# A gated convolution-and-MLP kernel: an early first sine, its constants in five tasks, the gate as columns of the array, the last matrix by transfer, and four outputs finished from PSUM

## The chip, the cores and the metric

The kernel runs on one core of one Trainium2 chip. The core has TensorE (PE; its weight loads are shown apart as PEld), VectorE (DVE), ScalarE (ACT), GpSimd (POOL) and SyncE (SP), which here issues all the transfers. SBUF is the working memory of 128 partitions, PSUM the memory that PE writes to, here eight banks of 512 fp32 columns. The metric is the device time of one execution in microseconds (us), and the median of the runs counts.

## The reference

Everything works on x = A_q, 2048 tokens of 640 columns in bf16. Two branches, A and B, are mixed by a gate per token:

```python
g = sigmoid((x * gate_w).sum(-1, keepdims=True))
out = g * A(x, k, v, ...) + (1 - g) * B(x, w1, w2, w3, w4)
```

Branch A: k is shifted by 0 to 3 tokens with four weights per column and summed, multiplied by v (this is kv), and convolved along the tokens with a filter of 2048 taps per column, ssm_k, by FFTs of length 4096; kv * ssm_D is added, and the sum is multiplied by x. Branch B: layernorm, w1 (640 to 640), gelu; the four quarters of the result are shifted by 1, -1, 2 and -2 tokens; w2; the residual is added (x1). Then layernorm, w3 (640 to 1536), gelu, w4 (1536 to 640), and x1 is added.

## The kernel before

**Tasks and their order.** `build` makes 769 tasks. Each has a name, an engine or a choice of two, a function that issues its instructions, the tasks it depends on, and the buffers it takes and gives back (banks of PSUM, the pools "xn", "FS", "FX", "GX", "Q", "O", "V" and others). The text ORDER lists the tasks by number; a letter behind a number names the engine (a for ACT, v for DVE, p for POOL). The tasks are issued in that order, so it fixes the order on each engine and in SP's queue of transfers. `place` goes through the list once with the durations written at the tasks, and decides which buffer a task gets and how many filler matmuls (L256, on zeros, their result is not used) stand ahead of a PE task. The hardware waits for what a task needs, not for the planned times.

**Layout.** A token is 32 n + 16 g + s: s counts 16 blocks of 128 tokens. x lies in SBUF as 16 such blocks and is overwritten by x1 and at last by branch B's result.

**Start.** POOL writes integer ramps (task `iota`, L392), then ones, a constant and the identity matrix, and zeroes one row of K (task `ident`, L403). DVE works out the phases of all cosines and sines as integers (`phsmall`, `phase0`, `phase1`, `phand`, L417 to L456), and one ACT instruction makes TRIG from them (`sin`, L458). SP loads x, the filter (SK) and weights. For each block of x the statistics are made on DVE or ACT (`st1`), finished on POOL (`rs1`, L530), the block is normalised (`nm1`) and transposed on PE in pairs of blocks (`tr1`, L548) into xnT. PE also transposes the filter in five blocks of 32 (`trh`, L762, evicted by `evt`), and broadcasts the four shift weights over the partitions (`cjb`, L473).

**Branch B.** W1 (`w1`, L623 and L627), gelu (`g1`, L640), W2 (`w2`, L649), the residual on DVE (`x1`, L656) with its sums on ACT (`sq`), the second layernorm (`ve2` on DVE, `st2` on POOL, `nm2`), a transposing transfer per block (`dt2`, L724), W3 in four groups of four blocks (`w3`, L732, 12 pieces each), gelu (`g2`, L739), W4 (`w4`, L746: 24 matmuls per block into two banks) and the sum into x on DVE (`t2`, L752). The later parts of groups 1 to 3 serve PE as work between the steps of branch A.

**Gate.** `gate` (L666) runs 80 matmuls of one column, five per block of tokens, and five for the sum of gate_w. `gz` (L677) undoes the layernorm for the product on DVE, a tanh and `gg` turn it into the two factors GG and OG per token.

**Branch A.** `kv` (L779 to L790): 8 DVE operations on 2560 columns for each of four groups of blocks, after which group K holds the product. The FFT is written as matmuls with TRIG. Step 1 (`s1h` for the filter, `s1x` for kv, L817 and L830) goes to the buffer FS (ACT or DVE, L387 and L389) and to DRAM (FH, FXD); kv group 0 is the last to be done, its step 1 has four blocks and a rest (`s1x.0` to `s1x.3`, `s1xr.0`). Then, ten times: load FX, step 2 for both (`s2`, L864), evict, products on DVE (L879), step 3 (`s3`, L892), evict to GS, store to GD. The last step (`s4`, L936) loads GX and needs the matrix BT: TRIG's rows are reordered into BP (part of the buffer XB) by DVE (`bperm`, L910), transposed by 16 matmuls (`trb`, L917) and copied back from PSUM by DVE (`evb`).

**Output.** For a block: `yq` (L942) takes step 4 from PSUM, multiplies by GG and by x as loaded anew (QO), into a piece of W4's buffer; `ad` (L948) adds x (by then branch B's result) times OG; two blocks are stored together in two halves of 64 partitions (`st`, L382).

Of the kernel before, what the change touches and what calls it, by code (L numbers as in the profile page):

```python
# [36 lines left out]
0 60v 22 73a 1 74 7 2 21 20 23 71v 3 8 4 9 16 72 63a 5 64 61a 53v 70p 14 51v 62 12 54 79v 13a 75v 31 36 52 18 38  # L37
391 81v 6 66v 56v 24 17a 392v 32 82 89v 25 65a 15a 395 80 67 76v 30 34 90 396a 69v 387 388v 55v 77 37 83v 68a
393 47 35 57 78a 87a 84v 88 28 26 394v 389 97v 33 85 59a 86v 390v 92v 119 42 10 397 121 58a 98 27 95v 100v 113v
19 450 41 91a 93 94v 96 40 11a 99v 111v 39 400 120 451a 123 122 438 124 105v 439a 29 444 43 127 452 401 402 445a  # L40
440 441a 141 101 145 125 112 115v 398 128 102a 453a 142 146 44 149 150 442 446 106 126 443a 147 148 403 404 129
130 447a 454 405 143 114 138 139 455a 132 133 45 144 406 103a 154 155 456 458 399 157 116a 131 407 50 457a 104
107v 158 448 160 161 459a 411 449 108a 134 135 109 136 117 140 151 152 110a 118a 211 137 410 412 163 212 164 462
464 460 468 465a 463a 165 217 167 185 213v 469a 186 169 408 413 470 218 46 466 215v 409 168 221v 414 166 415 416
417 171 467a 471a 461 193 49 474 170 214 473 172 478 187 191 479a 176 177 421 472 194 475a 173 216 192 219a 480
174 220 188 420 482 189 481a 190 179 222 180 476 483a 477a 485 156 204 422 486 494 205 423 201 202 484 207 495a
490 492 424 48 208 487a 418 162 153 419 425 491a 488 489a 493a 223 496 198 224 498 199 497 500 501a 231 239 426
502 504 499a 506 232 243 503a 233 240 225 431 507a 182 427 430 432 505a 433 226 244 510 234 514 428 515a 509 183
241 434 435 436 227 511a 242 228 429 512 516 513a 518 517a 519a 508 437 237 245 238 246 255 256 209 229 195 522
524 230 235 520 196 523v 525a 236 528 529a 530 526 249 521 253 257v 531a 527v 694v 210 251 247 159 206 258 178  # L50
533 261 250 532 184 203 259v 262 260 175 265v 263v 266 264 267 197 299 252 300 181 305 306 539 540 534 254 349
200 542 343 301a 309v 248 273 555 550 307v 541v 302 571 535 268 543a 537 274 538a 287 288 556 557a 536v 279 280
582 558 544 545 551 553 559a 552v 554a 310 289 290 281 308 572 566 303v 304 344 546 573a 547a 275 583 350 351v
574 276 560 548v 347v 575a 695 561 271 598 567 584a 696v 569 353v 585 282 603 283 570v 568a 586a 311 277 604 284
606 272 576 577 599 312 607v 315 605a 587 588 278 600v 590 589a 323 578 316 549 619 591v 324 580a 601 319 614
329 602a 320 635 630 592 562 593 269 579v 330 620 564v 563a 270 678 581 345v 608 609 615 622 621a 616v 325 623a
285 326 662 286 594 596a 565 331 631 595v 617 618v 327 636 637v 632a 633 332 624 634a 625 638 346 725 321 610
640 639a 667 641 612a 328 651 291 348 663 611a 322 664a 292 626 646 628a 665 313 627v 668 669v 666a 647 314 670
648v 671a 333 652 334 597 653v 654 655a 317 318 649 650a 642 644a 672 673 656 683 339 684 657 354 643a 613 340
674 679 676v 685a 681 352 645 675a 682v 658 680a 688 686 687a 660a 337 629 689 690 659a 335 661 677 338 692v 336  # L60
691a 693 297 707 724 341 342 298 295 706 355 356 726 708 296 727 709 729 365 730 369 742 728 366 697 370 361 733
# [293 lines left out]
def build(env, nc, io):  # L355
# [36 lines left out]
    def c_iota(t):  # L392
        T = env.early("TT", [P, 16, 2], I32)
        for h in range(2):
            nc.gpsimd.iota(T[64 * h:64 * h + 64], pattern=[[1, 16], [-6144, 2]], base=6144 + 16 * h, channel_multiplier=32)
        nc.gpsimd.iota(env.early("KC", [P, 64], I32)[:], pattern=[[4, 64]], base=1, channel_multiplier=0)
        nc.gpsimd.iota(env.early("PI", [P, 1], I32)[:], pattern=[[0, 1]], base=0, channel_multiplier=1)
        nc.gpsimd.iota(env.early("K2", [P, 2, 32], I32)[:], pattern=[[0, 2], [1, 32]], base=0, channel_multiplier=0)
        nc.gpsimd.iota(env.early("N2", [P, 5, 16, 2], I32)[:], pattern=[[0, 5], [1, 16], [16, 2]], base=0, channel_multiplier=0)
        nc.gpsimd.iota(env.early("OF", [P, 5, 32], I32)[:], pattern=[[-2048, 5], [0, 32]], base=6144, channel_multiplier=0)  # L400
    add("iota", "POOL", 2.2, c_iota, w=["iota"], roles=("C0",))

    def c_id(t):  # L403
        I = env["ID"]
        nc.gpsimd.memset(env["ONE"][:], 1.0)
        nc.gpsimd.memset(env.early("NPI", [P, 1], F32)[:], float(-np.pi * (1 - 2.0 ** -20)))
        nc.gpsimd.memset(I[:], 0.0)
        nc.gpsimd.affine_select(out=I[:], in_=I[:], compare_op=ALU.not_equal, fill=1.0, base=0, pattern=[[-1, P]],
                                channel_multiplier=1)
        nc.gpsimd.memset(env.sm("MH", [P, 2])[:], -0.5)  # L410
        nc.gpsimd.memset(env["K"][0:1, 0:3, :], 0.0)
    add("ident", "POOL", 2.9, c_id, w=["ID", "c0", ("K", "z")], roles=("C0", "K"))
# [27 lines left out]
    add("phsmall", "DVE", 2.6, c_small, r=["iota"], w=["ph0"], roles=("PRE", "C0"))  # L440
# [10 lines left out]
    for ri in range(2):  # L451
        add(f"phase{ri}", "DVE", 1.25, c_ph(ri), r=["iota"], w=[("ph", ri)], roles=("PRE", "C0"))
# [8 lines left out]
    add("sin", "ACT", 3.5, c_sin, r=["pha", "c0"], w=["TRIG"], roles=("PRE", "C0"))  # L461
# [203 lines left out]

    def gate(t):  # L666
        m = env.PS[:, t.buf["U"][0], :]
        gw = env.sm("GW", [P, 5], BF16)
        for s in range(16):
            for kb in range(5):  # L670
                nc.tensor.matmul(m[:, s:s + 1], lhsT=env["xnT"][:, s + 2, kb, :], rhs=gw[:, kb:kb + 1], start=(kb == 0),
                                 stop=(kb == 4))
        for kb in range(5):
            nc.tensor.matmul(m[:, 16:17], lhsT=env["ONE"][:], rhs=gw[:, kb:kb + 1], start=(kb == 0), stop=(kb == 4))
    tg = add("gate", "PE", 2.3, gate, r=["GW", "c0"] + [("xnT", s) for s in range(16)], acq=[ONE], mode="f", roles=("xnT",))

    def gz(t):  # L677
        m = env.PS[:, tg.buf["U"][0], :]
        z, sd = SS("Z"), SS("SD")
        sg = env.sm("SG", [P, 1])  # L680
        nc.vector.tensor_tensor(out=sd[:], in0=SS("VE")[:], in1=SS("RS")[:], op=ALU.mult)
        nc.vector.tensor_scalar(out=sg[:], in0=m[:, 16:17], scalar1=-1.0, scalar2=None, op0=ALU.mult)
        nc.vector.scalar_tensor_tensor(out=z[:], in0=SS("NB")[:], scalar=sg[:, 0:1], in1=m[:, 0:16], op0=ALU.mult, op1=ALU.add)
        nc.vector.tensor_tensor(out=z[:], in0=z[:], in1=sd[:], op=ALU.mult)
    add("gz", "DVE", 0.8, gz, use=[tg], rel=[(tg, "U")], r=[("RS", s) for s in range(16)], w=["Z"])
# [7 lines left out]
    add("gg", "DVE", 0.35, gg, r=["Z"], w=["GG"])  # L693
# [9 lines left out]
    def f_st2(t, s0):  # L703
        c = slice(s0, s0 + 2)
        r, nb = SS("r2")[:, c], SS("nb2")[:, c]
# [3 lines left out]

    for c in range(4):  # L710
        nT, nP = None, f"x1nT{c % 2}"
        for s0 in (4 * c, 4 * c + 2):
# [5 lines left out]
            for s in ss:  # L718
                def f_nm2(t, s=s):
                    k = slice(s, s + 1)  # L720
                    norm(t, env["xn"][:, t.buf["xn"][0], :], env["x"][:, s, :], SS("r2")[:, k], SS("nb2")[:, k])
# [19 lines left out]
        for s in range(4 * c, 4 * c + 4):  # L741
# [6 lines left out]
            t = add(f"w4.{s}", "PE", 3.28, w4, r=["W4"] + [("h2", c, fb) for fb in range(12)], rel=[(h2, "h2")], acq=("U",), mode="f")  # L748
# [165 lines left out]
    def trb(t):  # L914
        o = env.Ub(t.buf["U"][0])
        for s in range(16):
            nc.tensor.transpose(o[:, 128 * s:128 * s + 128], env.BP[:, s, :], env["ID"][:])  # L917
    tb = add("trb", "PE", 1.65, trb, r=["BP", "ID"], acq=("U",), mode="f")
    add("evb", {"ACT": 1.87, "DVE": 1.25}, 0, lambda t: copy(t, env["BT"].rearrange("p s t -> p (s t)"), env.Ub(tb.buf["U"][0])), use=[tb],
        rel=[(tb, "U")], w=["BT"])  # L920
    for s0 in range(0, 16, 2):
# [7 lines left out]
        for i in range(2):  # L929
# [16 lines left out]

            def ad(t_, s=s, i=i, y=y, o=oown):
# [5 lines left out]
            oown = oown or o  # L953
        halves(f"st.{s0}", P * 2 * D * BF * 1.3, lambda t, g, s0=s0: ov[g, :, s0:s0 + 2, :],
# [34 lines left out]
```

## Time and profile before

| | |
|---|---|
| median of 3 runs | 234.26 us (232.64 to 235.73) |
| the profiled execution | 233.85 us |
| its span in the profile | 232.1 us |
| mean granted TensorE clock | 0.988 |
| PE, DVE, ACT, POOL busy | 220.8, 186.9, 155.1, 40.5 us |
| moved by transfers | 56.23 MB, mean 242 GB/s |

A row of groups reads: line, engine, operation, output<-input by the program's names, shape, count, then busy time and mean ns of one, then the idle time of the engine just before such an instruction and what ended it. PE's matmuls overlap, so their mean is longer than the distance from one to the next; for PE the chain of waits is the better measure: it gives for each piece of work its start and the time until the next. "PE PS L746 x24" there means 24 matmuls of line 746 writing to PSUM. A row of waits tells who waited for whom, the total, how often, and the longest. In SP's rows "SPq" is the issue of a transfer, not the transfer.

### The profile page before, as it was taken

The page shows a single profiled execution, that of the slowest core. Times are in us where ns is not written, and L with a number is a line of the kernel's source. Part 1 is how long each engine was busy: PE and PEld are TensorE (multiplying, and loading weights), DVE is VectorE, ACT ScalarE, POOL GpSimd, SP SyncE. Part 2 cuts the span into 40 slices and gives each one's busy share as a digit, 9 for nine tenths or more (in the row PEclk, how much of TensorE's full clock was granted, in tenths as well). Part 3 has the DMA queues.
Part 4 walks back from the last instruction along what each step waited for, and adds up shares of the span by engine and source line. Part 5 has one row for each costly group of instructions (what it writes and reads, how often), then busy time and mean ns, then how long its engine had stood idle before and what let it go on. Part 6 is the DMA issues. An engine that isn't in the chain of part 4 may idle for free.

```text
span 232.1 us, 5340 instructions
## 1 busy us (share of the span) xinstructions
PE 220.8 (95%) x2143; PEld 108.6 (47%) x2163; DVE 186.9 (81%) x264; ACT 155.1 (67%) x221; POOL 40.5 (17%) x90
## 2 busy tenths in 40 slices
PE   7799999999999999999999999999999999999990
PEld 3158834456345744445543433344345554444550
DVE  5974699989999989997378998897986128887972
ACT  2996989988897998979669988888956004142000
POOL 7585317810700000011340000000000000000000
PEclk9979999999999999999999999999999999999998
DMA  5899889976999696867899995899843894968742
GB/s 149 280 277 303 198 237 272 330 270 206 289 294 283 196 266 224 270 224 250 191 315 300 327 349 177 255 228 310 204 172 135 242 406 147 282 187 248 233 109 57
DMA packets 39051, 56.23 MB, mean 242 GB/s; under 512 B 13809, under 2 KB 28914, under 8 KB 39026
## 3 DMA queue, kind: packets, MB, share of 16 engines
q1 hardware_dynamic: 39026, 55.88, 81.8%
q8 instruction: 17, 0.28, 0.5%
q14 instruction: 8, 0.07, 0.1%
HBM read 34.90 MB, written 18.35 MB: 229 GB/s over the span
## 4 chain that ended last, share of the span: by engine, by line
PE 80%; DVE 7%; DMA 4%; issue 2%; SPq 2%; ACT 2%; DVEq 0%; ACTq 0%
PE PS L746 21%; PE PS L732 18%; PE PS L649 8%; PE PS L623 7%; PE PS L864 4%; PE PS L892 4%; PE PS L762 3%; DMA FX<-FH 3%; PE PS L817 3%; DVE VC L786 3%; PE PS L256 2%; PE PS L936 2%; SPq L382 2%; PE PS L627 2%; DVE VC L782 2%
## 5 line engine op out<-in xcount | busy, mean ns | idle before, releaser
L746 PE MATMUL PS<-W,h2T 128*128 128x128 bf16 (+1 forms) x374 | 53.2, 297 | 0.5
L739 ACT ACTIVATE h2T<-PS 128x512 bf16<-128x512 f32 x48 | 28.1, 609 | 30.8 <-PE PS L732 30.0
L746 PEld LDWEIGHTS <-h2T 128*128 128x128 bf16 x384 | 29.6, 98 | 25.3 <-issue 2.5
L387 ACT CAST FS<-PS 128x1024 bf16<-128x1024 f32 x38 | 37.1, 1022 | 4.5 <-PE PS L817 2.6
L732 PEld LDWEIGHTS <-W 128*128 128x128 bf16 x240 | 21.2, 98 | 30.0 <-issue 8.5
L387 ACT CAST XH<-PS 128x1024 bf16<-128x1024 f32 x26 | 25.8, 1014 | 6.5 <-PE PS L864 6.4
L732 PE MATMUL PS<-x1nT,W 128*128 128x512 bf16 x120 | 28.8, 380 | 0.0
L732 PE MATMUL PS<-XB,W 128*128 128x512 bf16 x120 | 28.6, 380 | 0.0
L752 DVE TENSOR_TENSOR x<-PS,x 128x640 bf16<-128x640 f32 x16 | 13.1, 822 | 15.8 <-PE PS L746 15.8
L879 DVE TENSOR_TENSOR PP<-XH 128x2048 bf16<-128x2048 bf16 x20 | 23.6, 1219 | 0.9 <-PE PS L892 0.4
L782 DVE TENSOR_TENSOR VC<-K,VC 128x2560 bf16<-128x2560 bf16 x16 | 23.8, 1485 | 0.2
L649 PE MATMUL PS<-W,hsT 128*128 128x128 bf16 (+1 forms) x152 | 23.1, 295 | 0.4
L623 PE MATMUL PS<-xnT,W 128*128 128x512 bf16 x80 | 19.1, 380 | 0.5 <-ACT hsT L640 0.5
L389 DVE CAST XH<-PS 128x1024 bf16<-128x1024 f32 x14 | 16.7, 1219 | 2.8 <-PE PS L864 2.7
L649 PEld LDWEIGHTS <-hsT 128*128 128x128 bf16 x160 | 12.9, 98 | 11.5 <-issue 0.2
L786 DVE TENSOR_TENSOR VC<-VC 128x2560 bf16<-128x2560 bf16 x12 | 17.9, 1489 | 0.2
L942 DVE SCALAR_TENSOR_TENSOR W<-PS,GG,QO 128x640 bf16<-128x640 f32 x16 | 13.6, 879 | 4.4 <-PE PS L936 3.9
L706 POOL TENSOR_TENSOR r<-v,MH 128x2 f32<-128x2 f32 x8 | 6.9, 856 | 55.6 <-DVE v L701 55.5
L387 ACT CAST GS<-PS 128x1024 bf16<-128x1024 f32 x13 | 13.0, 1018 | 3.1 <-PE PS L892 3.1
L656 DVE SCALAR_TENSOR_TENSOR x<-PS,x 128x640 bf16<-128x640 f32 x16 | 13.1, 820 | 2.3 <-PE PS L649 2.0
L948 DVE SCALAR_TENSOR_TENSOR QO<-x,OG,W 128x640 bf16<-128x640 bf16 x16 | 13.6, 879 | 0.1
L864 PE MATMUL PS<-FX,TRIG 64*32 64x512 bf16 x320 | 12.9, 382 | 0.1
(106 smaller groups left out, 272.4 us busy)
## 6 DMA issues: line engine op xcount, KB each, us to landing
FH<-FS SPq DMA_DIRECT2D x8, 640.0 KB, 5.4
FXD<-FS SPq DMA_DIRECT2D x8, 640.0 KB, 4.6
FX<-FXD SPq DMA_DIRECT2D x10, 512.0 KB, 5.5
FX<-FH SPq DMA_DIRECT2D x10, 512.0 KB, 5.2
GX<-GD SPq DMA_DIRECT2D x8, 640.0 KB, 5.2
W<-in_B_w_dram SPq DMA_DIRECT2D x2, 1920.0 KB, 10.5
GD<-GS SPq DMA_DIRECT2D x8, 480.0 KB, 3.8
x<-in_A_q_dram SPq DMA_DIRECT2D x16, 160.0 KB, 4.9
```

Of the source, the lines that this page charges most:

```text
L387: nc.scalar.copy(out=out, in_=in_)
L389: (nc.vector if t.on == "DVE" else nc.gpsimd).tensor_copy(out=out, in_=in_)
L623: nc.tensor.matmul(m[:, b, :], lhsT=W[:, 0, kb, 160 * fb:160 * fb + 128], rhs=rhs(kb, shifts[fb]), start=(kb == 0), stop=(kb == 4))
L649: nc.tensor.matmul(m[:, c0:c1], lhsT=env["hsT"][:, o.buf["hs"][0], fb, 128 * (s % 4):128 * (s % 4) + 128], rhs=env["W12"][:, 1, fb, c0:c1] ...
L732: nc.tensor.matmul(env.PS[:, t.buf["U"][0], :], lhsT=env["W3"][:, kb, 128 * fb:128 * fb + 128], rhs=env.nT(int(nP[-1]))[:, :, kb, :], star ...
L739: nc.scalar.activation(out=env["h2T"][:, o.buf["h2"][0], fb, :], in_=env.PS[:, t.buf["U"][0], :], func=ACT.Gelu_apprx_tanh)
L746: nc.tensor.matmul(m[:, c0:c1], lhsT=env["h2T"][:, o.buf["h2"][0], fb, 128 * (s % 4):128 * (s % 4) + 128], rhs=env["W4"][:, fb, c0:c1], st ...
L782: nc.vector.tensor_tensor(out=VC[:, o], in0=env["K"][:, a + 3 - j:a + 7 - j, :], in1=w, op=ALU.mult)
L786: nc.vector.tensor_tensor(out=VC[:, 1], in0=VC[:, 1], in1=VC[:, 2], op=ALU.add)
L864: nc.tensor.matmul(env.U(t.buf["U"][0])[32 * j:32 * j + 32, gp, :], lhsT=CRI()[64 * gp:64 * gp + 64, 32 * pc:32 * pc + 32], rhs=X[64 * gp: ...
L879: nc.vector.tensor_tensor(out=env["PP"][:, o.buf["PP"][0], a, :].rearrange("p (b c) -> p b c", b=2), in0=X.unsqueeze(1).broadcast_to([P, 2 ...
L942: nc.vector.scalar_tensor_tensor(out=u, in0=env.Uf(t.buf["U"][0])[:, 0:D], scalar=SS("GG")[:, s:s + 1], in1=env["QO"][:, 2 * q.buf["Q"][0] ...
```

## The change

- **Sine.** DVE zeroes two elements (`warm0`) and ACT takes the sine of one of them (`warm`) as the first instruction of the kernel on ACT; `sin` comes after it.
- **Constants in five tasks.** `iota` keeps the ramps that `phase0` and `phase1` read; `iotb` holds the four others, which `phsmall` reads; `ident`, `ones` and `kz` hold the identity, the ones and constants, and the zero row of K.
- **Gate as array columns.** Five matmuls with one column each become one matmul of 5 columns for the sum of gate_w (`sgm`), reduced on DVE, which also copies gate_w over 32 columns (`sg`, GB). `gate` multiplies GB with xnT: 20 matmuls of 512 columns, four of them side by side in 32 output partitions each. `gz` gets the tokens back onto the partitions with two 32x32 block transposes on DVE out of PSUM.
- **Last matrix by transfer.** `bperm` may also run on POOL, and does in the new order; `trb` and `evb` are replaced by one transposing transfer of 16 blocks (`dbt`).
- **Last four outputs from PSUM.** For blocks 12 to 15, W4 is two tasks, 512 and 128 columns, one bank each. x1 times OG is added to the piece from `yq` first (`ax`), and then one DVE step for each half takes W4's result from PSUM, times OG, plus that piece, into the output (`fo`); `t2` and `ad` are not run for these blocks. Each of the four is stored by itself.
- **Order.** ORDER has 785 tasks and is another list throughout. Some tasks stand elsewhere: the shift weights are now the first transfer, the gate weights come behind two blocks of the filter, W3 is loaded ahead of W4, W4 behind the first stores to FXD, the gate runs among W1's second half. Ahead of the first transpose of the filter PE has 15 fillers.

```diff
-    add("iota", "POOL", 2.2, c_iota, w=["iota"], roles=("C0",))
+    add("iota", "POOL", 0.65, c_iota, w=["iota"], roles=("C0",))
...
+    def c_warm(t):
+
+        nc.vector.memset(env.sm("Z", [P, 16])[:, 0:2], 0.0)
+    add("warm0", "DVE", 0.08, c_warm, w=["WA"])
+    add("warm", "ACT", 1.5, lambda t: nc.scalar.activation(out=env.sm("Z", [P, 16])[:, 1:2], in_=env.sm("Z", [P, 16])[:, 0:1], func=ACT.Sin),
+        r=["WA"], w=["WB"])
...
-        for s in range(16):
-            for kb in range(5):
-                nc.tensor.matmul(m[:, s:s + 1], lhsT=env["xnT"][:, s + 2, kb, :], rhs=gw[:, kb:kb + 1], start=(kb == 0),
-                                 stop=(kb == 4))
+        gb = env.sm("GB", [P, 5, 32], BF16)
         for kb in range(5):
-            nc.tensor.matmul(m[:, 16:17], lhsT=env["ONE"][:], rhs=gw[:, kb:kb + 1], start=(kb == 0), stop=(kb == 4))
+            for k in range(4):
+                nc.tensor.matmul(m[32 * k:32 * k + 32, :], lhsT=gb[:, kb, :], rhs=env["xnT"][:, 2:18, kb, 32 * k:32 * k + 32],
+                                 start=(kb == 0), stop=(kb == 4))
...
+        for h in range(2):
+            nc.vector.transpose(out=T, in_=env.PS[:, tg.buf["U"][0], 256 * h:256 * h + 256])
+            c = slice(8 * h, 8 * h + 8)
+            nc.vector.tensor_tensor(out=z[:, c], in0=T.rearrange("p (s j) -> p s j", j=32)[:, :, 0], in1=z[:, c], op=ALU.subtract)
...
-    add("bperm", {"ACT": 2.5, "DVE": 1.4}, 0, lambda t: copy(
+    add("bperm", {"ACT": 2.5, "DVE": 1.4, "POOL": 3.5}, 0, lambda t: copy(
...
-        for s in range(16):
-            nc.tensor.transpose(o[:, 128 * s:128 * s + 128], env.BP[:, s, :], env["ID"][:])
...
+    dma("dbt", P * 2048 * BF * 1.8, lambda t: nc.sync.dma_start_transpose(
+        out=env["BT"][:], in_=env.BP.rearrange("p s t -> p (s t)")), issue=1.25, r=["BP"], w=["BT"])
...
+                    def fo(t_, s=s, i=i, y=y, o=oown, w=w, c0=c0, c1=c1):
+                        nc.vector.scalar_tensor_tensor(out=env["QO"][:, 4 + 2 * (o or t_).buf["O"][0] + i, c0:c1],
+                                                       in0=env.PS[:, w.buf["U"][0], 0:c1 - c0], scalar=SS("OG")[:, s:s + 1],
+                                                       in1=env["W4"][:, 12 + y.buf["V"][0], c0:c1], op0=ALU.mult, op1=ALU.add)
```

More of the change, by code (lines that the diff above doesn't have):

```diff
@@ L42 @@
[L42 to L46, printed above, removed]
@@ L451, in build @@
     for ri in range(2):
-        add(f"phase{ri}", "DVE", 1.25, c_ph(ri), r=["iota"], w=[("ph", ri)], roles=("PRE", "C0"))
+        add(f"phase{ri}", "DVE", 1.18, c_ph(ri), r=["iota"], w=[("ph", ri)], roles=("PRE", "C0"))
     def c_and(t):
@@ L684, in gz @@
         nc.vector.tensor_tensor(out=z[:], in0=z[:], in1=sd[:], op=ALU.mult)
-    add("gz", "DVE", 0.8, gz, use=[tg], rel=[(tg, "U")], r=[("RS", s) for s in range(16)], w=["Z"])
+    tz = add("gz", "DVE", 1.5, gz, use=[tg], rel=[(tg, "U")], r=[("RS", s) for s in range(16)] + ["SG"], w=["Z"], acq=("V",), after=("C0",))
     add("gtanh", "ACT", 0.25, lambda t: nc.scalar.activation(out=SS("Z")[:], in_=SS("Z")[:], func=ACT.Tanh, scale=0.5), r=["TRIG"], w=["Z"])
@@ L747, in w4, with w4n @@
                                          rhs=env["W4"][:, fb, c0:c1], start=(fb == 0), stop=(fb == 11))
-            t = add(f"w4.{s}", "PE", 3.28, w4, r=["W4"] + [("h2", c, fb) for fb in range(12)], rel=[(h2, "h2")], acq=("U",), mode="f")
+            kw = dict(r=["W4"] + [("h2", c, fb) for fb in range(12)], rel=[(h2, "h2")], mode="f")
+            if s in LATE:
+                for n, (c0, c1) in enumerate(((0, 512), (512, 640))):
+                    def w4n(t, c0=c0, c1=c1, s=s, o=h2):
+                        for fb in range(12):
+                            nc.tensor.matmul(env.PS[:, t.buf["U"][0], 0:c1 - c0], lhsT=env["h2T"][:, o.buf["h2"][0], fb, 128 * (s % 4):128 * (s % 4) + 128],
+                                             rhs=env["W4"][:, fb, c0:c1], start=(fb == 0), stop=(fb == 11))
+                    late[s, n] = add(f"w4.{s}.{n}", "PE", (2.62, 0.68)[n], w4n, acq=[ONE], **kw)
+                continue
+            t = add(f"w4.{s}", "PE", 3.28, w4, acq=("U",), **kw)
             def t2(t_, s=s, t=t):
```

109 lines of the change are left out of this document (68 added, 41 removed), and 8 rows, old and new, of the table ORDER.

## The prediction

> **What bounds the kernel now.** I read the page's busy line first, then PE's waits, then the busy time by stage, cut at three moments of the chain of waits: the first W1 matmul (28.75), the last block of the kv product (101.17) and the end of the last matmul (226.27).
>
> ```profile
> PE 220.8 (95%) x2143; PEld 108.6 (47%) x2163; DVE 186.9 (81%) x264; ACT 155.1 (67%) x221; POOL 40.5 (17%) x90
> ...
> PEclk9979999999999999999999999999999999999998
> ...
> PE PS L623 <- ACT hsT L640: 0.5, 1, 0.5
> ...
> 0.00:28.75 28.75, 25.50 (x243) 15.83 (x246) 19.74 (x50) 21.20 (x30) 17.13 (x51) 0.94 0.87 241
> 28.75:101.17 72.42, 71.38 (x608) 34.88 (x614) 68.99 (x95) 64.69 (x94) 16.68 (x22) 1.00 0.88 256
> 101.17:226.27 125.10, 123.88 (x1295) 57.95 (x1305) 96.42 (x118) 69.20 (x98) 6.70 (x18) 1.00 0.81 243
> 226.27:232.10 5.83, 0.00 (x0) 0.00 (x0) 1.71 (x2) 0.00 (x0) 0.00 (x0) 0.81 0.23 56
> ```
>
> The last four rows give, after the stretch and its length, PE, PEld, DVE, ACT and POOL busy, the TensorE clock, the DMA share and GB/s. From 28.75 to 226.27 PE rests 1.04 + 1.22 = 2.3 us of 197.5: there the kernel is a queue of matmuls, and only three things shorten it: less PE work, an earlier 28.75, a shorter tail after 226.27. The second row holds a rival bound: up to 101.17 DVE is busy 69.0 of 72.4 too.
>
> ```profile
> 11.76 2.25 PE PS L256 x5
> 14.01 1.92 PE PS L762 x27
> ...
> 16.08 1.67 PE PS L256 x7
> ...
> 28.75 1.08 PE PS L623 x5
> 29.83 0.67 PE PS L473 x2
> ...
> 34.95 1.19 PE PS L627 x20
> ...
> 79.13 1.98 PE PS L671 x80
> 81.11 0.12 PE PS L674 x5
> ...
> 99.62 1.50 DVE K L790
> 101.17 0.61 PE PS L817 x4
> ...
> 116.86 1.08 PE PS L732 x5
> ...
> 118.50 1.19 PE PS L732 x5
> ...
> 129.06 1.00 PE PS L917 x16
> ...
> 222.87 3.38 PE PS L746 x24
> 226.27 0.83 DVE x L752
> 227.13 0.89 DVE QO L948
> ```
>
> These are pieces of the chain of waits (start, length, what). At 101.17 PE starts on a block just when DVE's product at 99.62 is done (101.12): both engines arrive together.
>
> **The change, part by part.**
>
> *Start.* Before, the first spectral transpose (L762) runs at 14.01 and W1 starts 14.74 later. Five such blocks of 32 are 9.6 of it; the rest, 5.1, is the transposes of x, fillers (L256) and waits.
>
> ```profile
> 5.82 2.80 DMA C<-in_A_shift_k_dram
> ...
> 6.72 0.42 SPq L496 DMA_DIRECT2D SK<-in_A_ssm_k_dram  x1
> ...
> DMA to landing us min/median/max: 4.7/4.7/4.7
> ...
> 27.00:30.00 3.00, 3.00 (x36) 2.02 (x35) 1.84 (x5) 2.48 (x3) 1.38 (x5) 1.00 0.55 127
> ```
>
> The first SK block was issued at 6.72 and landed 4.7 later, at 11.4; in the new queue the same eight x halves and the shift row stand ahead of it, so 11.4 again. The shift row now goes first: issued at about 0.7, landed 2.8 later, 3.5. Four broadcasts of 0.67 with three pairs of fillers between (0.24 to 0.45 each by the two L256 rows, 2.4 for six) end at 8.3; 15 fillers follow, 3.6 to 6.8 us. The first transpose starts at 11.9 to 15.1; I take 13.0, between, because the filler price depends on the clock, which the page shows below full in the first slices (PEclk 9 and 7). Behind it stand 7 fillers instead of 11 (-1.0 to -1.8) and one new 5-column matmul (0.1, by L674): the stretch to W1 is 13.0 to 13.9 with its waits as they are, 12.2 if half of them go, 14.7 if the new matmul's wait for the gate weights takes the gain; I take 13.5: 26.5. W1's weights, landed by 28.75 before, have 0.56 MB less ahead (two x halves, one k block; 2.3 us at the 241 GB/s of the first stage), but the gate weights' 640 two-byte pieces move ahead of them; the row at 27.00, where these ran, shows the DMA share fall to 0.55, 1.4 us in three. That makes 27.9 at the latest, and likely not last. Start: -2.2 (bounds -4.6, the early ends of both; +1.0, the late ones). The Trainium skill, TensorE: Matmul & The Clock Gate, Part 1, says that PE falls to half clock after an idle window of some 3.4 us and needs as long to rise; by that rule alone all 15 fillers are slow if the pause for the shift row trips it, and the start comes at the late bound.
>
> The sine's table load leaves ACT's queue, the first sine on one element taking it while ACT waits for data, and DVE computes phases before x lands. Both feed the same start; I count nothing more. The constants' five tasks hold the same POOL instructions; only the zero row of K (1.69, L411 below) goes to a time when POOL rests. The table load was covered before too, since PE waited for no ACT instruction there but the 0.5 of L623.
>
> *Between W1 and 101.17.*
>
> ```profile
> L387 ACT CAST FS<-PS 128x1024 bf16<-128x1024 f32 x38 | 37.1, 1022 | 4.5 <-PE PS L817 2.6 <-issue 1.2 <-ACT h2T L739 0.4
> ...
> L942 DVE SCALAR_TENSOR_TENSOR W<-PS,GG,QO 128x640 bf16<-128x640 f32 x16 | 13.6, 879 | 4.4 <-PE PS L936 3.9 <-DMA QO<-in_A_q_dram 0.5
> ...
> L522 DVE BATCH_NORM_STATS2 BS<-x 128x6 f32<-128x128 bf16 x11 | 3.0, 275 | 0.0
> ```
>
> The gate's 85 matmuls (1.98 + 0.12) become 20 in the form of L627, 1.19: -0.91. The fourth broadcast has moved ahead of W1: -0.67. One W3 group more than before stands ahead of the block: +1.08 here and -1.08 later. A change of matmul form costs 0.11 (the two L732 rows), and the new order has 44 instead of 37 here: +0.77. Sum +0.27. DVE's work ahead of that block is the same 32 kv operations, with the gate's two 32x32 transposes out of PSUM new: no row has one; between 0.28 (128 columns, L522) and 0.88 (640 columns out of PSUM, L942) each; I take 0.4, as each moves 256 columns: 0.8 for both. DVE had 12.4 idle up to 101.17 (28.75 - 19.74 and 72.42 - 68.99), 9.0 of it in the first stage where it now works ahead, so it can follow. Block at 101.17 - 2.2 + 0.27 = 99.2.
>
> W3's load now comes before W4's, and W4's behind the first FXD stores. It is needed only behind the block at 101.17; 1.9 MB at that stage's 256 GB/s are 7.7 us, so issued by 85 it is in time; if not, each us late is one lost.
>
> *After it.* The 16 transposes at 129.06 go: -1.00, and the W3 group -1.08; one change of form less, -0.11. New: the last five s1x blocks follow each other without the W3 group that stood between them. Each leaves 1024 columns to be read by ACT or DVE, two engines for five reads of some 1.02, about 2.6 us, against 1.2 of PE work (0.61 for two, by the row at 101.17); that allows a PE wait of 0 to 1.4; I take 1.0, nearer the upper end because DVE has x additions queued there too. DVE sheds its two copies of the row matrix at no gain, since PE waited for neither. Sum -1.2.
>
> *Tail.* Before, the last matmul is followed by 0.83 + 0.89 on DVE, then the store.
>
> ```profile
> 228.04 1.11 SPq L382 DMA_DIRECT2D out_dram<-QO  x2
> ```
>
> After, the last PSUM piece has 128 columns: about 0.27 by L522 (bounds 0.18, L942 by columns, and 0.88). DVE's queue before it must also be done. From the first half of output 14 on it holds 5 steps of 0.84 (L942's 0.88, less overlap), 4 of 0.7 (512 of L942's 640 columns) and 4 of 0.27, 8.1 us; on PE stand two outputs of 24 matmuls (3.38 each by the row at 222.87), a fifth of another (0.7) and two small blocks (0.6), 8.1. So the result is ready 0.3 to 0.8 after the last matmul instead of 1.77: -1.3. The store is 80 KB halves instead of 160 (4.06 from issue to the end now): 0 to -0.5, I take -0.2.
>
> **The sum**: -2.2 + 0.27 - 1.2 - 1.5 = -4.6. The profiled execution took 233.85 (span 232.1 and 1.75 around it), so 229.2. It lies 0.41 under the median of 234.26, within the three runs' 232.64 to 235.73; about 2% is what a measurement of this kernel can tell from no change, and I leave the sum as it is.
>
> **What the cover hides.** The reordering of the row-matrix (BP) goes from DVE to POOL, and its transpose from PE to SP's queue.
>
> ```profile
> L411 POOL MEMSET K<- 1x1920 bf16 x1 | 1.7, 1688 | 0.0
> L399 POOL IOTA C<- 128x160 int32 x1 | 0.6, 573 | 0.0
> ...
> 36.02 1.49 DVE L782 TENSOR_TENSOR VC<-K,VC 128x2560 bf16<-128x2560 bf16 x1
> 36.04 1.55 POOL L534 TENSOR_SCALAR VE<-MV 128x1 f32<-128x1 f32 x1 [2.10 <-DVE MV L523]
> ...
> x1nT<-xn SPq DMA_TRANSPOSE x8, 6.1
> ...
> L724 SPq DMA_TRANSPOSE XB<-xn x4: 1236/1248/1637, 103.7 to 111.4; - x4
> ...
> DMA to landing us min/median/max: 2.6/2.6/2.7
> ...
> 183.42 10.22 SPq L924 DMA_DIRECT2D GX<-GD  x5
> 192.35 0.94 PE PS L936 x12
> ```
>
> A POOL copy of 2048 columns lies between 1.8 (0.88 ns a column, memset) and 7.3 (3.6, iota); I take 3.5, nearer the memset. Behind it in POOL's queue stand the statistics of the third group of rows, which PE needs some 20 us later: nothing on the path. The 16-block transpose lands between 2.6 us after its issue (five blocks, in the stretch from 103.7) and 3.2 times the slower five's 6.1, 19.5; I take 8.3, 3.2 times 2.6, and nothing needs it until the last stage at 192. Its issue occupies SP's queue for 1.2 to 4.0 (five blocks: 1.25).
>
> **The rivals.**
>
> *DVE sets the block at 101.17.* For it: DVE at 95% in that stage, and equal work. Against: 9.0 us of early idle time. Then the start and the gate give nothing: 229.2 + 1.9 = 231.1.
>
> *More at the start.* With the transpose at its early bound and no wait among the five blocks: 229.2 - 2.2 - 1.0 = 226.0. Against it: the x rows' statistics must follow on DVE.
>
> *POOL's copy holds DVE.* The rows at 36 show a POOL step on one column end 0.08 after DVE's product, which began with it. If it also works the other way, the normalisations next on DVE wait for the copy, then their transfers, then W3's second group at 116.86, with about 2.8 us of slack (the transpose issued at 111.4 lands 2.6 later, at 114.0). Price: copy less 2.8, up to 4.5; 229.2 + 2 = 231.2. The Trainium skill, SBUF — State Buffer, Who interferes with whom, states this as a rule: whichever of the two starts first holds the shared ports for its whole instruction. By it this rival would decide whenever the copy is issued first.
>
> *The matrix transfer blocks the queue (slower).* It stands in SP's queue among the stores of G and the last FX load. These share the DMA engines, and the last G store leads to the GX loads at 183.42, landed some 5.2 later, 3.7 before PE takes them. If it holds the others up for longer than 3.7, the rest is lost one for one: slower than before from a hold of 3.7 + 4.6 = 8.3 us; at 15 us, 229.2 + 11.3 = 240.5. Against it: its issue takes 4.0 at most, and a landing is time shared with the others.
>
> That the change does not do what it says I exclude but for the gain of the split tail, which is in the bounds.
>
> **How the numbers follow.** Forecast 0.50, DVE at the block 0.19, more at the start 0.12, POOL holding DVE 0.09, the matrix transfer 0.10. The bounds of the start (2.4 earlier, 3.2 later) and of the tail (0.5) make the range 226.0 to 233.0; beyond it lie the transfer rival and about half of the early case. Faster by over 2% is below 229.6: three fifths of the forecast, the early case and some of the rest, 0.48; slower by over 2% is above 238.9, the transfer rival with a hold of over 13.4: 0.08; within 2% the rest, 0.44.
>
> **What would show it.** First W1 matmul near 26.5 (right: 24 to 28); one stretch of 1.2 us for the gate; no L917 row; the s1x block near 99.2 and PE waits of about 1 us on the reads behind it; last matmul near 223.1 and a DVE step of 0.3 behind it, the store within 0.8. The forecast is wrong if PE shows new waits of more than 2 us between 28 and 223, if the POOL copy takes over 6 us with DVE idle beside it, or if a G store lands late behind the matrix transfer.

## The result, and the profile after

The changed kernel takes 232.14 us (median of 16 runs, 231.4 to 232.9); the kernel before, on the same chips, 234.25 (16 runs, 232.51 to 236.68). The ratio of the means, which leaves out three executions of the kernel before above 236 us, is 0.9928, 95% interval 0.9903 to 0.9953: 1.7 us faster, where 4.6 were forecast, and within the 2% that stand for no change.

Part of that is the clock granted to TensorE: of 46 executions of the kernel before that were taken beside the experiments, 13 lie at 232.4 to 232.7 us with a mean clock of 0.994 to 0.996, and 30 at 233.2 or more with 0.991 or less (the profiled one, 233.85 at 0.988, is like these), while all 16 of the changed kernel stand at 0.999 or 1.000. Against the 13 the change gives only about 0.4 us.

The profiled execution took 232.78, its span is 231.0. The clock row of the changed kernel's page:

```profile
PEclk9999999999999999999999999999999999999999
```

Busy time by stage, cut at the same three moments as before: the first W1 matmul, the first `s1x` block of group 0, the end of the last matmul. After the stretch and its length come PE, PEld, DVE, ACT and POOL busy, the clock, the DMA share and GB/s:

```profile
0.00:28.02 28.02, 26.75 (x242) 15.46 (x243) 20.45 (x50) 18.93 (x28) 14.61 (x48) 1.00 0.88 275
28.02:102.58 74.56, 72.59 (x557) 33.20 (x555) 70.79 (x99) 67.19 (x100) 21.81 (x28) 1.00 0.84 245
102.58:226.81 124.23, 122.70 (x1285) 56.38 (x1284) 99.13 (x121) 67.89 (x96) 8.15 (x16) 1.00 0.86 245
226.81:231.00 4.19, 0.00 (x1) 0.00 (x0) 0.57 (x2) 0.00 (x0) 0.00 (x0) 1.00 0.32 78
```

The four stretches were 28.75, 72.42, 125.10 and 5.83 before. So the start gave 0.73, the second stretch took 2.14 more, the third gave 0.87, the tail 1.64: together -1.10, which is the difference of the two profiled executions (-1.07). Against the forecast, the third stretch and the tail are right within 0.4; the start lacks 1.5 and the second stretch 1.9. These two are what has to be explained.

The start of the kernel before is no clean measure either. In its profiled execution the clock fell to 0.5 there, in the same kind of row:

```profile
11.50:13.00 1.50, 1.50 (x6) 0.47 (x5) 1.47 (x5) 1.18 (x2) 1.23 (x4) 0.50 1.07 242
13.00:14.50 1.50, 1.50 (x13) 0.66 (x13) 1.22 (x4) 1.49 (x2) 1.18 (x5) 0.50 1.11 251
```

The five fillers at 11.76 took 0.45 each, those at 16.08 0.24, so by these two rows of the chain the start cost about 1.0 us more than at full clock (an estimate; no trace of an execution of the kernel before with a higher clock was kept). The 0.73 is measured against that start.

The chain of waits of the changed kernel, at the start (start, length, what):

```profile
1.76 1.18 POOL ID L409
...
3.15 0.72 PE PS L487 x2
3.88 0.97 PE PS L256 x2
4.84 0.65 PE PS L487 x2
...
8.74 5.80 PE PS L256 x15
14.54 1.92 PE PS L796 x32
```

PE never rests between 3.15 and 27.5. The broadcasts (now L487) begin at 3.15, when POOL's constants are there, and take about 0.65 a pair, as the forecast had it; the pairs of fillers between them take 0.97, the slow price, and the last broadcast ends at 8.74. Then the 15 fillers take 5.80, and the first spectral transpose (now L796) comes at 14.54, not earlier than before (14.01). How the fillers run, from the groups of line 256 between 10.78 and 12.06, and from 12.91 on (the mean of one overlaps the next; 634 ns go with a distance of 0.43 from one to the next, 379 with 0.22):

```profile
L256 PE MATMUL PS<-C x4: 634/634/634, 10.8 to 12.1; 128*128 128x512 bf16 x4
...
L256 PE MATMUL PS<-C x5: 379/380/634, 12.9 to 14.2; 128*128 128x512 bf16 x5
```

Eleven of the 15, up to 13.3, run at the slow price, although the page's clock row shows full speed throughout.

PE's waits in the changed kernel:

```profile
PE PS L864 <- DVE x L670: 0.9, 1, 0.9
PE PS L637 <- ACT hsT L654: 0.7, 1, 0.7
PE PS L851 <- DVE x L670: 0.5, 2, 0.4
PE PS L864 <- DVE FS L389: 0.5, 1, 0.5
PE PS L637 <- DVE x L670: 0.3, 1, 0.3
```

The second row of L864 and the one of L851, 1.0 together, are those forecast among the five `s1x` blocks. The 0.7 stands at W1 and was 0.5 before. The 0.9 and the 0.3 are new; they lie between 70 and 72, and the timeline there, over all engines, shows what they come from (start, length, engine, line; in brackets the idle time before):

```profile
68.24 1.69 POOL L418 MEMSET K<- 1x1920 bf16 x1
68.33 1.78 DVE L556 TENSOR_SCALAR xn<-x,r,SB 128x640 bf16<-128x640 bf16 x1 [0.40 <-POOL SB L732]
...
70.90 0.40 PE L864 MATMUL PS<-HT,TRIG 64*128 64x128 bf16 x8 [0.91 <-DVE x L670]
...
71.64 1.24 PE L637 MATMUL PS<-xnT,W 128*128 128x512 bf16 x5 [0.34 <-DVE x L670]
```

POOL's zero row of K, which stood among the first constants before, now runs at 68.24. A normalisation on DVE that takes 0.44 elsewhere began 0.09 later, took 1.78 and ended 0.18 after it. The three x additions behind it on DVE came 1.3 late; they free the PSUM buffers of W2, and PE waited for those.

The tail of the changed kernel, from the timeline:

```profile
220.12 6.69 PE L778 MATMUL PS<-W,h2T 128*128 128x512 bf16 x48
...
226.37 1.01 DVE L984 SCALAR_TENSOR_TENSOR QO<-PS,OG,W 128x512 bf16<-128x512 f32 x2
```

The last matmul ends at 226.81, DVE's two steps at 227.38: 0.57 behind it.

### The profile page after: what moved, and what is told of

Same layout as the page of the kernel before. It is cut to its first block, busy times and chain, and to the rows that moved or that the text cites. A ratio compares the mean times of both kernels' runs of the same rounds, so it can differ in the third digit from the quotient of the medians.

```text
span 231.0 us, 5209 instructions
## 1 busy us (share of the span) xinstructions
PE 222.0 (96%) x2077; PEld 105.0 (45%) x2077; DVE 190.9 (83%) x269; ACT 154.0 (67%) x223; POOL 44.6 (19%) x92
## 4 chain that ended last, share of the span: by engine, by line
PE 89%; DVE 5%; ACT 2%; POOL 1%; issue 1%; DVEq 0%; POOLq 0%; ACTq 0%
PE PS L757 24%; PE PS L771 17%; PE PS L663 10%; PE PS L637 7%; PE PS L898 5%; PE PS L256 5%; PE PS L796 4%; PE PS L926 4%; PE PS L851 3%; PE PS L778 3%; PE PS L641 2%; PE PS L964 2%; PE PS L562 1%; DVE QO L984 1%; PE PS L487 1%; DVE W L978 1%
## 5 line engine op out<-in xcount | busy, mean ns | idle before, releaser
L771 PE MATMUL PS<-W,h2T 128*128 128x512 bf16 (+1 forms) x288 | 40.1, 299 | 0.0
L771 PEld LDWEIGHTS <-h2T 128*128 128x128 bf16 x288 | 22.2, 98 | 18.8 <-issue 1.5
L387 ACT CAST XH<-PS 128x1024 bf16<-128x1024 f32 x24 | 23.9, 1014 | 8.2 <-PE PS L898 7.4
L663 PE MATMUL PS<-W,hsT 128*128 128x512 bf16 (+1 forms) x160 | 23.2, 299 | 0.0
L389 DVE CAST XH<-PS 128x1024 bf16<-128x1024 f32 x16 | 19.4, 1221 | 3.0 <-PE PS L898 2.5
L786 DVE TENSOR_TENSOR x<-PS,x 128x640 bf16<-128x640 f32 x12 | 9.6, 821 | 11.6 <-PE PS L771 11.5
L730 POOL TENSOR_TENSOR r<-v,MH 128x2 f32<-128x2 f32 x8 | 8.2, 1021 | 54.8 <-DVE v L725 52.1
L256 PE MATMUL PS<-C 128*128 128x512 bf16 x32 | 13.0, 548 | 1.2 <-DVE C L477 1.2
L654 ACT ACTIVATE hsT<-PS 128x512 bf16<-128x512 f32 x20 | 11.6, 609 | 3.8 <-PE PS L637 2.4
L778 PE MATMUL PS<-W,h2T 128*128 128x128 bf16 (+1 forms) x96 | 13.6, 299 | 0.0
```

What stands on the lines that cost most here:

```text
L256: nc.tensor.matmul(env.PS[:, t.fill_at, :], lhsT=Z[:, 0:128], rhs=Z[:], start=True, stop=True)
L387: nc.scalar.copy(out=out, in_=in_)
L389: (nc.vector if t.on == "DVE" else nc.gpsimd).tensor_copy(out=out, in_=in_)
L663: nc.tensor.matmul(m[:, c0:c1], lhsT=env["hsT"][:, o.buf["hs"][0], fb, 128 * (s % 4):128 * (s % 4) + 128], rhs=env["W12"][:, 1, fb, c0:c1] ...
L771: nc.tensor.matmul(m[:, c0:c1], lhsT=env["h2T"][:, o.buf["h2"][0], fb, 128 * (s % 4):128 * (s % 4) + 128], rhs=env["W4"][:, fb, c0:c1], st ...
L778: nc.tensor.matmul(env.PS[:, t.buf["U"][0], 0:c1 - c0], lhsT=env["h2T"][:, o.buf["h2"][0], fb, 128 * (s % 4):128 * (s % 4) + 128], rhs=env ...
```

## The experiments

The theory after this reading: the start lost its gain to 15 fillers at the slow price, and the second stretch lost most of its own to the zero row of K, which holds DVE. The rivals: data, not fillers, set the first W1 matmul; and the stall on DVE is covered, or DVE's kv products set the block anyway. Four kernels on one chip tell them apart; the kernel before took 234.26 there. All edits are to the changed kernel.

**Fewer fillers ahead of the first transpose.**

```diff
+CAP = {'trh.3': 6}
...
-                for _ in range(t.fill):
+                for _ in range(CAP.get(t.name, t.fill)):
```

> The changed kernel with 6 fillers instead of 15 ahead of the first spectral transpose, nothing else. In the changed kernel PE runs without a pause from 1.2 to 27.5, and these 15 take 5.80 us, the first 10 of them at the slow price of 0.43. Theory (PE's own queue sets the start, and DVE, which waited 5.9 us for these transposes, follows): the transpose starts at 8.74 + 6 x 0.43 = 11.3, 3.2 earlier, some of it lost since the first transposes run slowly; first W1 matmul at 25.5 instead of 28.0, the s1x block at 100 instead of 102.6, time 229.6. Rival (statistics and normalisation of x, or W1's weights, set the first W1 matmul): new PE waits of 2 to 3 us before 28, first W1 matmul at 27.5 or later, time 231.6 or more.

230.16 us, ratio to the kernel before 0.9862 (0.9797 to 0.9927). The chain of waits of this kernel:

```profile
8.73 2.67 PE PS L256 x6
11.41 1.93 PE PS L796 x32
```

The first W1 matmul starts at 25.0, the `s1x` block at 99.5: both 3.1 earlier, with no new wait on PE ahead of them, and the last matmul ends 2.6 earlier. DVE and ACT followed at once; the theory holds. The transposes behind six slow fillers took 1.93 for 32, as much as any later, so the loss that was expected for a slow first block isn't there.

**The zero row of K at the start.**

```diff
-0 5 14 12 26 28 25 2 8 9 3 1 7 10
+0 5 14 12 26 28 25 2 8 9 3 1 4p 7 10
...
-493 4p 427
+493 427
```

> The changed kernel with POOL's zero row of K written at the start, behind the constants, instead of at 68.24; nothing else. In the changed kernel DVE's normalisation that began at 68.33 took 1.78 us beside that memset of 1.69, and PE waited 0.9 and 0.3 for the x additions behind it. Theory (POOL's memset holds DVE, and DVE sets the s1x block): the normalisation takes 0.44, DVE's last kv product ends 1.3 earlier, the s1x block at 101.3 instead of 102.6, time 231.0. Rival (the stall is covered, PE's queue or a later wait sets the block): the normalisation takes 0.44 and the block and the time stay, 102.6 and 232.1.

231.12 us, ratio 0.9885 (0.9833 to 0.9936). DVE in this kernel, from the timeline:

```profile
68.30 0.45 DVE L556 TENSOR_SCALAR xn<-x,r,SB 128x640 bf16<-128x640 bf16 x1 [0.40 <-POOL SB L732]
68.66 0.82 DVE L670 SCALAR_TENSOR_TENSOR x<-PS,x 128x640 bf16<-128x640 f32 x1
```

The normalisation takes 0.45; among PE's waits the 0.9 and the 0.3 at 70 are gone; the block starts 1.35 earlier (101.16 against 102.51 in the timelines) with the same first W1 matmul. POOL's memset held DVE.

**Both.** CAP as in the first, ORDER as in the second.

> Both edits together: 6 fillers ahead of the first transpose, and the zero row of K at the start. If the two losses lie one behind the other on the same chain, they add: s1x block at 98.7, time 228.4. If DVE's queue of kv products alone sets the block, and starts no earlier with fewer fillers, the time is that of the memset edit alone, 231.0.

228.63 us, ratio 0.9808 (0.9729 to 0.9887), W1 at 25.2, the block at 98.3: the two losses add. This is 0.6 under what was forecast for the change itself.

**Both, and none of the later fillers.**

```diff
-CAP = {'trh.3': 6}
+CAP = {'trh.3': 6, 'tr1.14': 0, 'tr1.0': 0, 'tr1.2': 0, 'trh.4': 0}
```

> As the one with both edits, and also without the 7 fillers that stand among the transposes of x and the last filter block (1.7 us of PE time in the changed kernel). If PE's queue still sets the first W1 matmul, it comes up to 1.5 earlier than with both edits, and the time is 227 to 227.5; if data set it by then, PE waits in their place and the time is that of both edits, within 0.4.

228.55 us, ratio 0.9789 (0.9734 to 0.9844). The waits of PE in this kernel have a new row:

```profile
PE PS L637 <- DMA W<-in_B_w_dram: 0.5, 1, 0.5
```

W1 starts at 24.5, having waited for its weights: from here the data set the start. The block still comes 0.7 earlier than with both edits (97.65), but behind it PE waits 0.4 for a load of FX, the last matmul ends only 0.1 earlier, and the time is that of both edits.

Four more on another chip take the parts of the change back one at a time (the kernel before 233.58 there), and ask why the fillers were slow.

**The tail as before.** With `LATE` empty, W4, `t2` and `ad` for all blocks, stored in pairs:

```diff
-    LATE, late = (12, 13, 14, 15), {}
+    LATE, late = (), {}
```

> The changed kernel with the tail as before: for the last four blocks W4 into two banks, the sum into x, then the output step, stored in pairs. Theory (the two DVE steps and the larger store stand behind the last matmul): from the last matmul to the end 5.8 us instead of 4.2, time 233.7. Rival (DVE is the late engine at the end, or the last store of one block costs as much as one of two): 5.8 is not reached, time 232.1 to 232.8.

235.63 us, ratio 1.0089 (1.0063 to 1.0115): 3.5 more than the changed kernel, twice what was expected. The order of the changed kernel doesn't suit the old tail, as DVE's end in this kernel shows:

```profile
226.79 0.88 DVE L996 SCALAR_TENSOR_TENSOR QO<-x,OG,W 128x640 bf16<-128x640 bf16 x1 [1.49 <-DMA out_dram<-QO]
227.59 0.88 DVE L970 SCALAR_TENSOR_TENSOR W<-PS,GG,QO 128x640 bf16<-128x640 f32 x1
228.38 0.82 DVE L786 TENSOR_TENSOR x<-PS,x 128x640 bf16<-128x640 f32 x1
```

An output step waits 1.49 for a store to free its buffer, and the steps behind the last matmul come late. So 3.5 is no price of the tail alone; the two traces give 1.64 for it. Neither expectation holds.

**The gate as before.** `sgm` and `sg` left out, `gate` and `gz` from the kernel before; CAP holds the fillers of one task at two.

> The changed kernel with the gate as before: 85 matmuls of one column and the shorter work on DVE. PE has 0.9 us more, DVE about 1.4 less (2.1 for the five matmul columns' sum, the copy over 32 columns and the two block transposes with what lies around them, against 0.7). Theory (DVE sets the s1x block): the block comes at 101.5 to 102.6 though PE has more to do, time 231.3 to 232.1. Rival (PE sets it): the block at 103.5, time 233.0.

232.37 us, ratio 0.9966 (0.9922 to 1.0010). In the profiled execution the fillers happened to turn fast earlier (15 in 4.6 us instead of 5.8) and W1 started at 26.6; from there the block took 75.4 against 74.5. That is PE's 0.9, in spite of 1.4 us less on DVE, which waits 1.7 us for a W2 result at 63.4 instead: PE's queue sets the block. The time itself can't tell, since the start differs.

**The last matrix as before.** `trb` and `evb` in the place of `dbt`, `bperm` on DVE.

> The changed kernel with the last matrix as before: reordered by DVE, transposed by 16 matmuls, copied back by DVE, at the place of the transfer. Theory (PE works without a pause there, the transfer is hidden): PE has 1.0 to 1.1 more, time 233.2. Rival (the transfer holds back others in the queue, or POOL's copy, beside which three normalisations on DVE took 2.86 instead of 1.2, costs as much): 232.1 or less.

233.88 us, ratio 1.0018 (0.9989 to 1.0047), 1.7 more than the changed kernel's 232.14 on other chips; its profile has the 16 transposes as one piece of 1.00, and from the block to the end of the last matmul 1.2 more than the changed kernel. The rivals fall: the transfer and POOL's copy cost nothing that comes near PE's 1.0.

**The same fillers, nine of them ahead of the first broadcast.**

```diff
+CAP = {'trh.3': 6, 'cjb.0': 13}
```

> The changed kernel with the same number of fillers, 9 of the 15 moved ahead of the first broadcast. In the changed kernel fillers take 0.43 apiece until 12.9 though the granted clock is 1.00, while before they were at full speed from 4.6. Theory (the one-row broadcasts between pairs of fillers keep PE slow; 3.4 us of fillers alone make it fast): 8 fillers at 0.43, then 0.22, the broadcasts half as long; transposes from 11 on (waiting for data), first W1 matmul at 25.0, time 229.8. Rival (the first 13 us are slow whatever PE does): 13 fillers at 0.43, first transpose at 14.5, time 232.1.

232.33 us, ratio 0.9940 (0.9903 to 0.9977). PE in this kernel, from the timeline, and then two rows of its busy time by window:

```profile
1.21 4.42 PE L256 MATMUL PS<-C 128*128 128x512 bf16 x13 [1.21 <-DVE C L477]
...
9.78 1.47 PE L256 MATMUL PS<-C 128*128 128x512 bf16 x6
11.32 1.99 PE L796 MATMUL PS<-ID,SK 128*64 128x128 bf16 x32
14.05 0.17 PE L682 MATMUL PS<-GW,ONE 128*128 128x5 bf16 x1 [0.74 <-DMA GW<-in_gate_w_dram]
```

```profile
14.00:15.00 1.00, 0.95 (x17) 0.85 (x16) 0.84 (x1) 1.00 (x3) 0.10 (x1) 0.70 1.03 277
15.00:16.00 1.00, 1.00 (x22) 1.00 (x19) 0.00 (x0) 1.00 (x2) 0.81 (x3) 0.50 0.94 326
```

The first half of the theory holds: 13 fillers alone take 4.35 (7 at 0.43 and 6 at 0.22 make 4.3), so they are fast from about 4.2, the later six take 1.3, and the transposes begin at 11.3. The broadcasts are not half as long, though: a pair still takes 0.65. The second half doesn't hold: after a wait of 0.74 for the gate weights the granted clock falls to 0.5 for 3.4 us from about 14.4, and W1 comes at 26.6 instead of 25.0. Of the 3.2 us gained at the transposes 1.5 are left at W1. The profiled execution (231.29) keeps them, but the eight executions reach up to 234.18, with mean clocks from 0.985 to 1.000, and their median shows no gain.

The last four, on a third chip (the kernel before 233.72), build on the kernel with both edits.

**Gelu's table earlier.**

```diff
+    add("warmg", "ACT", 1.5, lambda t: nc.scalar.activation(out=env.sm("Z", [P, 16])[:, 2:3], in_=env.sm("Z", [P, 16])[:, 0:1], func=ACT.Gelu_apprx_tanh), r=["WA", "TRIG"], w=["WG"])
```

CAP also keeps out the fillers that `place` would add at three tasks because of the new one.

> The kernel with both edits (6 fillers, zero row of K at the start), and a gelu of one element on ACT behind the normalisation of block 5, where ACT rested 1.17 us, so that gelu's table (1.28) is loaded before W1's first result is there. Theory (the 0.7 us that PE waited for the first gelu, behind the table load at 27.87, is on the path): that wait goes, time 0.5 to 0.7 under the kernel with both edits, 228.0. Rival (ACT then copies xnT 0.3 later and W1 waits for that, or later waits take it up): 228.4 to 228.9.

> The same without the 7 later fillers. There the first W1 matmul waited 0.5 for W1's weights (24.5), so the gelu's table is what is left to gain: 227.7 to 228.0; if the weights and the table end together, no more than the kernel without the later fillers, 228.5.

230.19 us, ratio 0.9828 (0.9775 to 0.9881), and without the later fillers 229.37, ratio 0.9829 (0.9780 to 0.9879). In the profiled execution of the first (227.72) PE's wait of 0.7 is gone and the way from W1 to the block is 72.3 instead of 73.2, as the theory has it. But of its six executions only two, 227.72 and 228.26, have a mean granted clock of 0.996 or more; the others, 229.99 to 230.54, stand at 0.989 to 0.991. So the table's 0.7 is there, and is lost again where the clock falls. Why it falls in more executions here than there isn't settled; the chips differ too.

The second has 228.48 and 228.66 at 1.000 and the rest between 229.3 and 230.92, so even at full clock it gains nothing over 228.55. The profiled execution (228.66) has a new wait ahead of the first W1 matmul:

```profile
PE PS L637 <- issue: 0.9, 1, 0.9
```

The profile names no releaser. But the table load now holds ACT from 22.43 to 23.71, ACT's copies of xnT behind it end at 25.09, and W1 starts at 25.2, 0.6 later than without the early gelu, which is what the wait for the first gelu was (0.63). By these times the rival holds here: ACT copies later, and W1 waits for that.

**The gate as before, on the kernel with both edits.**

> The kernel with both edits, with the gate as before (85 matmuls of one column, the shorter work on DVE). Its start does not hang on when PE becomes fast, so the two gates can be compared. PE has 0.9 more ahead of the s1x block, DVE 1.4 less. If PE's queue sets the block (in the kernel with the old gate and the long start it took 75.4 from the first W1 matmul to the block against 74.5): block 0.9 later than 98.3, time 229.5. If DVE sets it: block and time 0 to 1 earlier, 228.0 to 228.6.

231.24 us, ratio 0.9886 (0.9836 to 0.9937), from 229.5 to 232.29. Its profiled execution, busy time by window and the chain of waits around the gate (L685, L688):

```profile
50.00:55.00 5.00, 4.95 (x114) 3.64 (x112) 4.67 (x11) 3.91 (x6) 2.11 (x3) 1.00 0.89 207
55.00:60.00 5.00, 5.00 (x32) 1.76 (x32) 4.88 (x6) 3.74 (x5) 0.16 (x1) 0.66 0.84 281
```

```profile
52.53 2.08 PE PS L685 x80
54.61 0.12 PE PS L688 x5
...
55.27 3.95 PE PS L637 x10
```

Behind the one-column matmuls the clock falls to a mean of 0.66 for 5 us, and ten W1 matmuls take 3.95, which take 2.26 at 57.10 in the chain of the changed kernel. From W1 to the block it is 75.7 against 73.2: 0.9 for the gate itself, some 1.6 for the clock. Two executions with a clock of 1.000, 229.5 and 229.66, are what the first case gave, and PE sets the block; a third with that clock took 232.29, which stays unexplained, and the fall of the clock was in neither case.

**No first sine, on the kernel with both edits.** `warm0` and `warm` left out.

> The kernel with both edits without the sine of one element, so the sine's table (1.28) is loaded ahead of the large sine at 9.4. If ACT has room (it rested 0.65 at 17.2 and 1.17 at 22.6): time as with both edits, 228.6, at most 0.4 more. If ACT's copies of xnT set the first W1 matmul: that one 1.0 to 1.3 later, time 229.8.

229.60 us, ratio 0.9845 (0.9800 to 0.9890). Five of six executions lie at 229.5 to 230.0; three of four with the sine lay at 228.4 to 228.7. That speaks for the second expectation, 1.0 us, but on another chip and with intervals that overlap; the profiled execution is the sixth (231.47, with PE waits of 0.9 and 0.5 for transfers and a clock of 0.5 from 17 to 20) and can't show it.

## Why the prediction was wrong, point by point

- **Start, -2.2 forecast, -0.7 measured.** The step that failed is "I take 13.0, between, because the filler price depends on the clock": 11 of 15 fillers ran at 0.43, the transpose started at 14.54, near the late bound of 15.1. A smaller slip lies ahead of it: 3.5, four broadcasts of 0.67 and 2.4 for the six fillers between add up to 8.6, not 8.3 (measured 8.74). The rest of the step is right: from there to W1 13.48, forecast 13.5. The first experiment gives the lost time back by taking fillers away. The 28.75 that all of this is counted from had lost about 1.0 us to half clock itself (above).
- **What the Trainium skill said of it.** TensorE: Matmul & The Clock Gate, Part 1, gave the late bound by a pause for the shift row. The outcome agrees, the reason doesn't: PE paused 0.3 us ahead of the broadcasts and not at all after 3.15. With one-row broadcasts between pairs of fillers it stayed slow up to 8.74, and the fillers behind them needed another 4.7 us (2.5 in the profiled execution of the kernel with the old gate, whose start is nearly the same). Fillers alone made it fast in 3.0 us (the experiment with nine of them first) and 3.4 us (the kernel before), about the page's time of some 3.4.
- **Second stretch, +0.27 forecast, +2.14 measured.** The step that failed is the sentence that the zero row of K "goes to a time when POOL rests", costed at nothing: POOL rested, but DVE didn't. It cost 1.35 (second experiment). The same rows at 36 were used for a rival about POOL's copy, and not held against this memset. Of the 0.5 left, 0.2 is the longer wait for the first gelu; 0.3 isn't settled. The gate's own term (-0.91) is right: one stretch of 1.19 in the chain, and 0.9 lost when it was put back.
- **DVE sets the block (rival).** The time came near its 231.1, but not by its mechanism: PE reached the block without waiting for kv, and with 1.4 us less DVE work the way to the block was no shorter. DVE is close behind, though: in the changed kernel its last product ends 0.2 us before the block starts, and it never rests from 68.3 on, so by these rows PE work saved behind 68 would soon wait for DVE (not tried).

```profile
100.80 1.49 DVE L824 TENSOR_TENSOR K<-VC 128x2560 bf16<-128x2560 bf16 x1
...
102.51 0.39 PE L851 MATMUL PS<-K,TRIG 64*128 64x512 bf16 x2
```

- **POOL's copy holds DVE (rival).** The mechanism is right, the price nothing. The changed kernel's timeline:

```profile
106.55 2.49 POOL L389 COPY XB<-TRIG 128x2048 bf16<-128x2048 bf16 x1
...
107.07 2.86 DVE L556 TENSOR_SCALAR xn<-x,r,SB 128x640 bf16<-128x640 bf16 x3
```

  Three normalisations took 2.86; with the copy on DVE 1.16. PE had 96 W4 matmuls to run and waited for none of it. The Trainium skill, SBUF — State Buffer, Who interferes with whom, has the rule (the one that starts first keeps the shared ports for its whole instruction), and the trace agrees at 68.24, where the normalisation ended 0.18 after the memset, and here, where the three ended 0.89 after the copy.
- **The matrix transfer (rival).** The rows of its line in the changed kernel, the issue in ns and the landing in us:

```profile
L947 SPq DMA_TRANSPOSE BT<-XB x1: 6678/6678/6678, 154.7 to 154.7; - x1
...
DMA to landing us min/median/max: 8.8/8.8/8.8
```

  It landed in 8.8 (taken: 8.3). Its issue held SP's queue for 6.68, over the bound of 4.0, and still PE waited for no transfer behind it. The 16 transposes were worth their 1.0 at least (1.7 when put back).
- **After the block, -1.2 forecast, -0.87 measured;** the waits among the five blocks are 1.05, forecast 1.0. **Tail, -1.5 forecast, -1.64 measured;** result ready 0.57 behind the last matmul, forecast 0.3 to 0.8.
- **The range** (226.0 to 233.0) holds the time; the forecast itself needed both failed steps to be right, as the kernel with both edits shows (228.63).

## What to carry to other kernels

A filler ahead of work that sets the start is work: count its price at the slow clock, and keep no more than cover the wait for data. Before a small POOL instruction is moved, look at what DVE runs at the new place, not at whether POOL is free there; a 1.7 us memset of one row cost PE 1.3 us through DVE and the PSUM buffers. Compare executions at the same granted clock before a gain of 1% is credited to a change: here 1.7 us shrink to about 0.4. And when one term of a profile row has been used for one rival, go through every other instruction of the change that the row applies to.

## What the runs showed of the hardware

- PE can be slow while the granted clock in the profile reads 1.00: fillers stood 0.43 apart until 13.3 in the changed kernel. The distance between matmuls tells it, the clock row didn't.
- Being busy isn't enough to be fast. One-row broadcasts between pairs of fillers left PE slow for the 5.6 us that they took, though it never rested; behind 85 one-column matmuls, PE busy 4.95 of 5.00 us, the clock fell to a mean of 0.66 for 5 us in one execution (in the profiled ones of the kernel before and of the other kernel with the old gate it didn't). Whether those matmuls brought the fall is not shown: without them, in the kernel with the earlier gelu, four of six executions have a mean clock of 0.989 to 0.991.
- The spectral transposes cost 1.92 to 1.93 for 32 right behind slow fillers as well as later, and 1.92 at 14.01 in the kernel before, where the granted clock was 0.5 for the first 0.8 us.
- Once fast, PE can lose it again in the start: the clock fell to 0.5 for 3.4 us in the kernel with nine fillers first. Whether the broadcasts, the transposes or the wait of 0.74 brought it, no run tells apart. It also fell within 3 us behind PE waits of 1.74 (the kernel before) and 0.94 (no first sine), but a wait of 0.91 at 70 in the changed kernel brought no fall.
- A POOL memset of a single row of 1920 columns (1.69 us) stretched a DVE normalisation of 128x640 that began 0.09 later from 0.45 to 1.78 us; a POOL copy of 128x2048 (2.49 us) stretched three of them from 1.16 to 2.86.
